# Moving the single-tile case to the head of each expert's code in a routed MoE kernel

## The chip, the core and the metric

## The reference

Attention over 8 batches with 8 heads (keys and values pooled by 8) gives 4608 rows of 512; each row is then sent to one of 8 experts.

```
scores = scale * np.matmul(q, k_p.transpose(0, 1, 3, 2))
...
logits = x @ w_gate
e_idx = np.argmax(logits, axis=1)
...
for e in range(E):
    mask = e_idx == e
    ...
    h = np.maximum(x[mask] @ w1[e], 0.0)
    ye = h @ w2[e]
    out[mask] = gate_w[mask, None] * eom[mask, e, None] * ye
```

w1[e] is 512 x 1024, w2[e] is 1024 x 512. Which expert gets how many rows is known only at run time. With the inputs that are timed the experts e0 to e7 get 1018, 55, 333, 239, 827, 724, 24 and 1388 rows, that is 8, 1, 3, 2, 7, 6, 1 and 11 tiles of 128 rows.

## The kernel before

Attention and routing take the first 176 us or so. At their end DVE works out a small integer table from the counts (`job_table`, L700): for each expert how many jobs of three tiles (trips) and of two tiles (pairs) it has, and some flags. Every engine then loads its words of this table and branches on them.

The experts run in order. A trip or a pair is one job: its tiles are transposed (PE's input `xt` is made by DVE from `turned`, high parts by ACT, low parts by DVE), PE runs the first layer (`l1`, L1055, weights `w1a` or `w1b`) and the second layer (L1032, weights `w2a` or `w2b`), DVE and ACT make `ht` between them, and DVE scales the result to `rows` (L1306). The letters a and b are two buffers that alternate between experts: e0, e2, e4, e6 use a for w1 and w2, the odd experts use b. Weights come in chunks to `stage` and are split into a high and a low part by ACT (L1171) and DVE (L1284, a `TENSOR_TENSOR` of 128x1024 each); this goes on during the jobs of the expert before.

An expert with one tile is a lone tile. If it has at most 64 rows, it is also "halved": high and low parts share one tile (`stack`, L1328, copies the low part beside the high one), the weights are the moving operand (L1064), the sums are turned back by PE (L1070), DVE adds halves (L1337) and makes the low part (L1341), the second layer has 16 matmuls (L1041), and DVE ends with three operations (`y_part`, L1299 to L1303). With these inputs e1 and e6 are halved lone tiles. The last tile's scaling of a job (`last_output`, L1308) is done by DVE at the head of the next job, before its first low part `low` of `ht` (L1317), which PE waits for in the second half of `l1`: four of the eight slices of `p_h` fit, the fifth needs the first `ht`.

The code of an expert is written out once per expert for DVE, ACT and POOL; PE has one copy for e0 and one loop over the pairs e1, e2; e3, e4; e5, e6; e7. An expert's code holds first the loop over trips and then the loop over pairs, and the lone tile's code lies inside the pairs' body, behind its `If`s. A lone tile therefore jumps over the trips. PE has three static hints that a branch's target will be needed (`BRANCH_PREFETCH_HINT`); DVE and ACT have none. In a lone tile the split of the weights that come next is done in part before the sums (`AHEAD[1]` chunks, L64) and the rest after the `xt` of the next job (`rest`, L900).

## Time and profile before

| what | value |
|---|---|
| median of 3 runs | 604.85 us (603.19 to 605.37) |
| the profiled execution | 606.75 us, its span 605.0 us |
| PE busy | 570.1 us, 94% of the span |
| DVE, ACT, POOL busy | 362.5, 256.5, 224.2 us |
| mean granted clock of PE | 0.994 |

The span is the time between the first and the last recorded instruction of the profiled execution; 1.75 us of its time lie outside. Times of rows are counted from the span's start. An idle time in brackets stands ahead of the instruction and names what ended it; "issue" means that the engine waited for nothing that the profile shows, so for its own sequencer.

### The profile page before, as it was taken

What the parts mean: (1) busy time and instruction counts of PE and PEld (TensorE: products, weight loads), DVE (VectorE), ACT (ScalarE), POOL (GpSimd) and SP (SyncE); (2) the same over time, 40 slices, a digit from 0 to 9 for tenths busy, and PEclk for the clock granted to TensorE, in tenths of its full rate; (3) what the DMA queues carried; (4) which work ended last, traced back from release to release, by engine and by line L of the source; (5) the groups of instructions that cost most, each with busy time, mean ns of one, the idle gap of its engine ahead of it and who ended that gap; (6) DMA issues with size and microseconds to landing.
All of it is one profiled execution on the core that took longest, in us unless ns stands there. A gap on an engine that the chain in (4) does not pass through costs nothing.

```text
span 605.0 us, 11705 instructions
## 1 busy us (share of the span) xinstructions
PE 570.1 (94%) x3331; PEld 510.9 (84%) x3331; DVE 362.5 (60%) x880; ACT 256.5 (42%) x701; POOL 224.2 (37%) x331
## 2 busy tenths in 40 slices
PE   2998999999999999879999999999999899999996
PEld 2898898888878989579889898998997788989895
DVE  6788899988978625678586423574254652232323
ACT  2897888788525204438254111542041420302120
POOL 2958879851634312144123131222112431213121
PEclk9999999999999999979999999999999999999999
DMA  8766888976567443678666203372125202010110
GB/s 333 301 250 266 349 309 306 382 293 150 187 205 192 155 105 113 180 208 273 195 234 207 62 36 73 109 231 55 52 87 144 62 16 77 8 52 19 35 36 35
DMA packets 44682, 96.59 MB, mean 160 GB/s; under 512 B 5515, under 2 KB 28475, under 8 KB 41664
## 3 DMA queue, kind: packets, MB, share of 16 engines
q1 hardware_dynamic: 29328, 48.95, 25.2%
q10 hardware_dynamic: 7488, 27.27, 13.6%
q0 software_dynamic: 7792, 19.61, 9.2%
q14 instruction: 55, 0.45, 0.2%
q8 instruction: 19, 0.31, 0.2%
HBM read 76.36 MB, written 22.91 MB: 164 GB/s over the span
## 4 chain that ended last, share of the span: by engine, by line
PE 62%; issue 3%; DVE 2%; DVEq 1%; DMA 1%; SPq 1%; ACT 1%; POOL 0%; ACTq 0%; POOLq 0%
PE p_h L1055 31%; PE p_y L1032 30%; DMA rows<-xs 1%; PE p_h L1064 1%; DVE turned L1260 0%; DVE w2b L1284 0%; DVE q_even L1337 0%; PE p_h L1070 0%; DVE w2a L1284 0%; DVE xt L1256 0%; DVEq L1309 0%; SPq L988 0%; ACT xt L1160 0%; ACT q_even L1193 0%; DVE rows L1306 0%
## 5 line engine op out<-in xcount | busy, mean ns | idle before, releaser
L1182 ACT ACTIVATE ht<-p_h 128x384 fp32r<-128x384 f32 (+1 forms) x104 | 46.8, 450 | 253.2 <-PE p_h L1055 250.8
L1483 POOL DMA_INDIRECT out<-rows,dst x41 | 42.9, 1045 | 217.1 <-DVE rows L1306 209.4
L1317 DVE SCALAR_TENSOR_TENSOR ht<-p_h,ht 128x384 fp32r<-128x384 f32 (+1 forms) x104 | 52.2, 504 | 97.3 <-ACT ht L1182 97.3
L1055 PE MATMUL p_h<-xt,w1b 128*128 128x384 f32 (+1 forms) x672 | 107.5, 321 | 1.0 <-DVE ht L1317 0.6
L1055 PEld LDWEIGHTS p_h<-xt,w1b 128*128 128x128 f32 x672 | 106.3, 188 | 2.3 <-DVE ht L1317 0.9
L1032 PE MATMUL p_y<-w2b,ht 128*128 128x512 f32 x456 | 107.4, 395 | 0.0
L1032 PEld LDWEIGHTS p_y<-w2b,ht 128*128 128x128 f32 x456 | 85.4, 188 | 20.1
L1055 PE MATMUL p_h<-xt,w1a 128*128 128x384 f32 (+1 forms) x576 | 88.3, 315 | 4.3 <-issue 3.9
L1055 PEld LDWEIGHTS p_h<-xt,w1a 128*128 128x128 f32 x576 | 87.5, 194 | 5.5 <-issue 4.3
L1032 PE MATMUL p_y<-w2a,ht 128*128 128x512 f32 x384 | 88.4, 390 | 0.0
L1032 PEld LDWEIGHTS p_y<-w2a,ht 128*128 128x128 f32 x384 | 71.9, 188 | 14.6
L1306 DVE TENSOR_SCALAR rows<-p_y,sc 128x512 f32<-128x512 f32 x39 | 28.9, 744 | 86.8 <-PE p_y L1032 77.0
L289 ACT ACTIVATE p<-p_h,m 128x72 f32<-128x72 f32 x288 | 69.7, 346 | 16.6 <-DVE m L283 16.2
L311 PE MATMUL p_y<-vbd,pT 128*128 128x162 f32 (+3 forms) x400 | 68.8, 320 | 5.8 <-DVE xg L334 4.1
L1458 POOL DMA_INDIRECT rows<-xs,src x51 | 55.5, 1089 | 24.9 <-POOL src L1454 13.5
L311 PEld LDWEIGHTS p_y<-vbd,pT 128*128 128x128 f32 (+1 forms) x400 | 54.2, 180 | 11.2 <-issue 3.7
L446 POOL DMA_INDIRECT xs<-xg,where x36 | 36.8, 1022 | 39.2 <-DVE grec L328 19.3
L203 POOL TENSOR_TENSOR kq<-kq 128x288 f32<-128x288 f32 (+1 forms) x63 | 42.3, 677 | 16.8 <-DMA kq<-kT 11.4
L277 PE MATMUL p_h<-kbd,q_even 128*128 128x144 f32 (+1 forms) x160 | 29.6, 315 | 11.5 <-DMA q_even<-qT 8.8
L334 DVE TENSOR_TENSOR xg<-p_y,grec 128x240 f32<-128x240 f32 x72 | 35.3, 490 | 1.4
L277 PEld LDWEIGHTS p_h<-kbd,q_even 128*128 128x128 f32 (+1 forms) x160 | 23.6, 197 | 13.9 <-issue 9.6
L1260 DVE STREAM_TRANSPOSE turned<-rows 128x512 f32<-128x512 f32 x51 | 32.4, 686 | 4.8 <-DMA rows<-xs 2.0
(190 smaller groups left out, 688.6 us busy)
## 6 DMA issues: line engine op xcount, KB each, us to landing
stage<-wst ACTq DMA_DIRECT2D x52, 512.0 KB, 4.3
rows<-v SPq DMA_DIRECT2D x8, 1280.0 KB, 6.4
kq<-kT SPq DMA_DIRECT2D x7, 1152.0 KB, 11.8
rows<-xs SPq DMA_DIRECT2D x36, 192.0 KB, 4.8
stage<-wst SPq DMA_DIRECT2D x12, 512.0 KB, 6.0
kq<-qT SPq DMA_DIRECT2D x4, 1152.0 KB, 9.4
q_even<-qT SPq DMA_DIRECT2D x3, 1152.0 KB, 10.3
rows<-xs SPq DMA_DIRECT2D x20, 128.0 KB
```

Source lines behind the costliest of these rows:

```text
L203: eng.tensor_tensor(k[:, :, 0:w], k[:, :, 0:w], k[:, :, w:2 * w], op=ALU.add)
L277: nc.tensor.matmul(s[r0:r0 + n, 144 * c:144 * c + 144], q_t[b][:, 2 * a + c, s0:s0 + n], kbd[b % 2][:, 2 * a + c, :], start=True, stop=True)
L289: nc.scalar.activation(pt[i % 3][:, o:o + KEYS], sv[:, h], AF.Exp, bias=m[:, h:h + 1])
L311: nc.tensor.matmul(av[r0:r0 + n, COLS * h:COLS * (h + n_heads)], pT[:, c, r0:r0 + n], vbd[b % 2][:, slot:slot + n_heads].rearrange("p h f ...
L334: nc.vector.tensor_tensor(xg[g][:, j, 0:LEAD + DM].rearrange("p (f h) -> p f h", h=H)[:, :, hs], avv[:, :, 0:GATE + D].rearrange("p h f -> ...
L446: ins = nc.gpsimd.indirect_dma_start(out=whole_rows(xs), out_offset=bass.IndirectOffsetOnAxis(ap=where, axis=0), in_=x.bitcast(I32), in_of ...
L1032: i = mm(to, ht[:, h, f, P * k:P * k + P], w[:, part, o:o + DM], start=(f == 0 and part == 0 and h == 0), stop=(f == 7 and h == 1))
L1055: i = mm(p_h[f % DEEP][:, 0:n], w[:, part, o:o + P], xt[:, x, d, 0:n], start=(d == 0 and part == 0 and x == 0), stop=(d == 3 and part == 1))
L1182: act(ht[:, 0, f, 0:size * P], p_h[f % DEEP][:, 0:size * P], AF.Relu).then_inc(q["hh"], 1)
L1317: nc.vector.scalar_tensor_tensor(ht[:, 1, f, 0:n], src, 0.0, ht[:, 0, f, 0:n].bitcast(F32), op0=ALU.max, op1=ALU.subtract).then_inc(q["hl" ...
L1458: nc.gpsimd.indirect_dma_start(out=xm[:, k].bitcast(I32), out_offset=None, in_=xs, in_offset=bass.IndirectOffsetOnAxis(ap=src[:, k:k + 1], ...
L1483: nc.gpsimd.indirect_dma_start(out=out, out_offset=bass.IndirectOffsetOnAxis(ap=dst[:, k:k + 1], axis=0), in_=yb[2 if k == size - 1 else k ...
```

## The change

For DVE, ACT and PE's looped experts an expert's code now begins with a branch on "lone": the lone tile's body stands there, its last jump goes to the end of the expert's code, and a hint for that jump's target stands at the start of the body. All experts with more tiles branch over the lone body to `many`, which holds trips and pairs. Five hints stand in PE's stream, eight each in DVE's and ACT's. `AHEAD[1]` falls from 2 to 1, `stack()` moves from the job before a lone tile to the lone tile's own start, a semaphore ("hv") is merged into another ("ad"), and the flag for at most 64 rows is made from the count alone, which drops `sh.halved` (32 bytes per partition) and some small steps of the table. The second weight buffers lie 32 bytes lower: `w1b` from 158112 to 158080, `w2b` from 190880 to 190848, while `w1a` (41600) and `w2a` (74368) stay.

```
-AHEAD = {3: 8, 2: 8, 1: 2}
+AHEAD = {3: 8, 2: 8, 1: 1}
...
+        few = t([P, E], F32, "few")
+        v_.tensor_scalar(few, cnt, float(P // 2), None, op0=ALU.is_le)
...
-        v_.scalar_tensor_tensor(spare, tiles, float(P), cnt, op0=ALU.mult, op1=ALU.subtract)
-        yield 0
-        v_.tensor_scalar(spare, spare, float(P // 2), float(HALF), op0=ALU.is_ge, op1=ALU.mult)
...
-        v_.scalar_tensor_tensor(sh.halved, sh.single, 0.0, spare, op0=ALU.is_gt, op1=ALU.mult)
+        v_.scalar_tensor_tensor(sh.single, few, float(HALF), sh.single, op0=ALU.mult, op1=ALU.add)
...
-    v_.tensor_tensor_scan(rest[:, ::-1], none[:, ::-1], sh.halved[:, ::-1], 0.0, op0=ALU.mult, op1=ALU.add)
     v_.tensor_tensor(table[:, E + 1:E + 2], after[:, 0:1], full, op=ALU.add)
     v_.memset(table[:, E:E + 1], 0)
-    yield 0
-    v_.tensor_tensor(pairs, pairs, sh.halved, op=ALU.add)
-    yield 0
-    v_.scalar_tensor_tensor(pairs[:, 0:E - 1], rest[:, 1:E], 2.0, pairs[:, 0:E - 1], op0=ALU.mult, op1=ALU.add)
...
+        if lone and not (lone == "half" and isinstance(e, int)):
+            name = f"lone_{nc.next_id()}"
+            branch = eng.br_cond((v & (HALF + 64)) <= HALF if lone == "half" else single <= 0, f"{name}_many", f"{name}_body")
+            if hint is not None and hint[LONE[1]] is not None:
+                branch.branch_hint(hint[LONE[1]])
+                hint[LONE[1]] = None
+            with nc.body(f"{name}_body", valid_engines=[eng.engine]):
+                end = eng.mark_branch_hint_location()
+                body(e, 2, job, slot, True if lone == "half" else v & HALF, 0, after_pairs, 1, late)
+                eng.br(f"{name}_end").branch_hint(end)
+            with nc.body(f"{name}_many", valid_engines=[eng.engine]):
+                many(job, slot)
+                eng.br(f"{name}_end")
+            nc.switch_bb(f"{name}_end")
+        else:
+            many(job, slot)
...
+            if e and single is not None:
+                with eng.If(single > 0):
+                    stack()
             with eng.If(job > 0):
                 last_output(u)
...
-            if e + 1 < E:
-                with eng.If(last * 1024 + halves[1] > 1024):
-                    stack()
...
-        sh.slots, sh.upto, sh.single, sh.halved = (sb(n, [P, E], F32) for n in ("slots", "upto", "single", "halved"))
+        sh.slots, sh.upto, sh.single = (sb(n, [P, E], F32) for n in ("slots", "upto", "single"))
```

The order of instructions at three places follows. The first is DVE's tail of e6's lone tile, between the `xt` of e7's first job and the turns for the one after it. Before, two chunks of weights are split there:

```order
L924 COMPARE_AND_BRANCH
L1284 TENSOR_TENSOR w2b<-stage2,w2b 128x1024
L1284 TENSOR_TENSOR w2b<-stage3,w2b 128x1024
L924 UNCONDITIONAL_BRANCH
L1266 ISA
```

In the changed kernel it is three (the line numbers are those of the changed kernel):

```order
L935 COMPARE_AND_BRANCH
L1295 TENSOR_TENSOR w2b<-stage1,w2b 128x1024
L1295 TENSOR_TENSOR w2b<-stage2,w2b 128x1024
L1295 TENSOR_TENSOR w2b<-stage3,w2b 128x1024
L935 UNCONDITIONAL_BRANCH
L1277 ISA
```

One split moved from in front of the halves' sums to this place; turns and `y_part` stand behind it.

The second place is DVE's way into e7 (L799 reads the expert's word, L781 branches to trips or past them, and L1306 is `last_output`). Before, the trips' code follows in line:

```order
L945 UNCONDITIONAL_BRANCH
L799 REGISTER_ALU x2
L781 COMPARE_AND_BRANCH
L807 UNCONDITIONAL_BRANCH
L807 ISA
L1355 ISA
L1355 COMPARE_AND_BRANCH
L1309 ISA x5
L1306 TENSOR_SCALAR rows<-p_y2,sc 128x512
```

In the changed kernel the word is read at L793, and L812 branches to `many`; between them and the trips stands the whole lone body, which begins like this:

```order
L962 UNCONDITIONAL_BRANCH
L793 REGISTER_ALU x2
L812 COMPARE_AND_BRANCH
L817 BRANCH_PREFETCH_HINT
L1367 REGISTER_ALU
L1367 COMPARE_AND_BRANCH
L1340 ISA x4
L1341 CAST xt<-xt 128x4x64
L1367 UNCONDITIONAL_BRANCH
```

An expert with many tiles now takes the branch L812 over that body. Counted by instruction addresses in the built program, e7's branch lies at about 2839 to 2860 and its `many` at 2920; e2's lie at 1276 to 1300 and 1371, and the lone tiles of e1 and e6 begin at 994 and 2549 in line with the expert before.

The third place is PE's head of a looped expert (the first of the two in an iteration). Before, trips follow the header:

```order
L781 COMPARE_AND_BRANCH
L807 UNCONDITIONAL_BRANCH
L807 ISA
L1023 ISA
L1055 MATMUL p_h0<-xt,w1b 128x384 x12
```

In the changed kernel the lone tile follows it:

```order
L812 COMPARE_AND_BRANCH
L817 BRANCH_PREFETCH_HINT
L1090 REGISTER_ALU
L1040 ISA
L1094 ISA
L1081 MATMUL p_h0<-w1b,xt 128x512 x8
```

PE's lone tile is entered without a jump, and a trip or pair lies further from the header than before.

## Rows read from the trace of the kernel before

**Rows 1.** The page, part 1: busy time and share of each engine
```profile
PE 570.1 (94%) x3331; PEld 510.9 (84%) x3331; DVE 362.5 (60%) x880; ACT 256.5 (42%) x701; POOL 224.2 (37%) x331
```

**Rows 2.** PE's timeline at e1 and e2: start, us, line, operation, [idle before]
```profile
246.86 2.82 PE L1064 MATMUL p_h<-w1b,xt 128*128 128x512 f32 x11 [1.58 <-issue]
...
252.18 0.66 PE L1070 MATMUL p_h<-ident,q_even 128*128 128x128 f32 x4 [0.69 <-ACT q_even L1193]
...
260.99 19.54 PE L1055 MATMUL p_h<-xt,w1a 128*128 128x384 f32 x96 [3.90 <-issue]
```

**Rows 3.** Windows at e1's end: us, busy times (x count), granted clock, DMA
```profile
257.00:259.00 2.00, 0.09 (x1) 0.00 (x0) 2.00 (x3) 0.56 (x1) 1.54 (x1) 1.00 0.95 389
...
260.00:266.00 6.00, 5.01 (x16) 5.01 (x17) 4.01 (x7) 0.77 (x2) 2.43 (x4) 0.50 0.67 140
```

**Rows 4.** PE's timeline: both layers of a trip with either buffer
```profile
335.96 16.52 PE L1032 MATMUL p_y<-w2a,ht 128*128 128x512 f32 x72
430.59 16.81 PE L1055 MATMUL p_h<-xt,w1b 128*128 128x384 f32 x96
447.24 16.95 PE L1032 MATMUL p_y<-w2b,ht 128*128 128x512 f32 x72
```

**Rows 5.** PE's timeline in the attention, an idle of middle length
```profile
12.78 2.29 PE L277 MATMUL p_h<-kbd,q_even 128*128 128x144 f32 x8 [2.73 <-ACT kbd L208]
```

**Rows 6.** PE's timeline at e6 and e7
```profile
464.03 2.68 PE L1064 MATMUL p_h<-w1a,xt 128*128 128x512 f32 x11
468.00 0.66 PE L1070 MATMUL p_h<-ident,q_even 128*128 128x128 f32 x4 [1.30 <-ACT q_even L1193]
...
470.89 0.66 PE L1070 MATMUL p_h<-ident,q_even 128*128 128x128 f32 x4 [1.07 <-ACT q_even L1193]
...
476.17 8.60 PE L1055 MATMUL p_h<-xt,w1b 128*128 128x384 f32 x48 [0.41 <-DVE xt L1256]
485.38 8.61 PE L1055 MATMUL p_h<-xt,w1b 128*128 128x384 f32 x48 [0.61 <-DVE ht L1317]
```

**Rows 7.** The chain of waits, e5 to e7: start, us, what (q: an engine's sequencer)
```profile
459.87 0.06 DVEq L781
459.93 4.25 issue
...
481.58 0.06 DVE rows L1303
...
482.39 0.04 DVEq L781
...
484.11 0.07 DVE rows L1306
```

**Rows 8.** DMA queues from 450 to 485 us: packets, MB, share
```profile
q14 instruction: 9, 0.07, 0.6%
```

**Rows 9.** The page, part 5: second-layer matmuls by weight buffer
```profile
L1032 PE MATMUL p_y<-w2b,ht 128*128 128x512 f32 x456 | 107.4, 395 | 0.0
L1032 PE MATMUL p_y<-w2a,ht 128*128 128x512 f32 x384 | 88.4, 390 | 0.0
```

**Rows 10.** DVE's timeline at the end of the job table
```profile
167.75 0.16 DVE L730 TENSOR_TENSOR jobs<-jobs,halved 128x8 f32<-128x8 f32 x1
...
167.95 0.17 DVE L732 SCALAR_TENSOR_TENSOR jobs<-jobs 128x7 f32<-128x7 f32 x1
```

**Rows 11.** DVE's timeline from e1's lone tile into e2
```profile
255.16 1.90 DVE L1256 TENSOR_TENSOR xt<-turned,xt 128x512 fp32r<-128x512 f32 x3 [0.49 <-ACT xt L1160]
256.98 2.35 DVE L1284 TENSOR_TENSOR w2a<-stage,w2a 128x1024 fp32r<-128x1024 f32 x2
...
262.63 0.49 DVE L1303 TENSOR_SCALAR rows<-rows,sc 64x512 f32<-64x512 f32 x1
264.30 0.75 DVE L1306 TENSOR_SCALAR rows<-p_y,sc 128x512 f32<-128x512 f32 x1 [1.19 <-issue]
265.75 0.56 DVE L1317 SCALAR_TENSOR_TENSOR ht<-p_h,ht 128x384 fp32r<-128x384 f32 x1 [0.70 <-ACT ht L1182]
```

## The prediction

> **What bounds the kernel now.** I read the page first: TensorE is busy for 570.1 us, 94% of the span [rows 1]. So only three things can move the time by much: the pace of its matmuls, its idle gaps, and its clock. Next I read PE's timeline around the two lone tiles, where the changed code lies. At e1 PE idles 1.58 us before its first matmul and, behind the lone tile, 3.90 us before e2's first layer, both ended by "issue", that is by its own sequencer [rows 2]. [...] e2's first 96 matmuls then take 19.54 us [rows 2], where the same number of the same form takes 16.81 [rows 4]: 2.73 us. A gap of 2.73 us elsewhere is followed by matmuls at their usual pace [rows 5]. At e6 and e7 the gaps are 1.30, 1.07, 0.41 and 0.61 us [rows 6].

> The chain of waits says why e6 is slow: DVE stands 4.25 us at the branch over the trips (L781) for nothing but its sequencer, while the same branch, when the target follows in line, takes 0.04 us [rows 7]. Instruction packets move in that stretch, nine with 0.07 MB [rows 8], so about 8 KB each. By addresses in the built program the long waits of DVE and ACT lie where a branch passes an address 64 past a multiple of 128, so I take a packet for a block of 128 instructions that begins there, and the 4.25 us for a branch into a block that has not arrived: at e6 DVE had entered the block that it leaves only half a microsecond before.

> **The change, part by part.**

> *Second weight buffers, 32 bytes lower.* The second layer reads w2b at 395 ns a matmul and w2a at 390 [rows 9]; for a trip's 72 matmuls that is 16.95 against 16.52 us, 0.43 or, with its neighbours, 0.42 us [rows 4], while the first layer shows no such difference. The buffers differ in address: w2a lies on a multiple of 128 bytes, w2b 32 bytes past one; after the change both lie on one. If that is the cause, 456 matmuls gain 456/72 x 0.42 = 2.66 us. Bounds: 0 (the cause is something else) and 2.7. I take 2.66, since nothing else in the two stretches differs.

> *Shorter table.* Two dependent steps go, of some 0.2 us each (167.75 to 167.95 is one) [rows 10], and five or so small operations of 0.16. It runs under attention's matmuls; what shows is the time at which the table can be loaded. Against it DVE and ACT now branch over e0's lone body. I take +0.2, bounds -0.3 and +0.5.

> *e1.* The lone tile is now in line behind e0 on PE, DVE and ACT, so the idle of 1.58 us [rows 2] goes and everything in e1 shifts by that. The lone tile's last jump is hinted, so the 3.90 us go too. PE could begin e2 when its xt is there: 255.16 + 1.90 - 1.58 = 255.48 [rows 11], with the branches about 256.4. After 48 matmuls (8.6 us, as the first half at e7 takes [rows 6]) it needs DVE's first ht, at 265.0.

> DVE is then the question. It has one split more behind the sums (AHEAD 1 instead of 2): 2.35/2 = 1.18 us [rows 11]. Its last y_part operation starts at 262.63 - 1.58 + 1.18 = 262.2; `last_output` follows 1.67 us later and takes 0.75, the first low part 0.56 [rows 11]: done about 265.2 by DVE alone, 266.2 with the longer header and ACT's part. PE would idle about 1.2 us.

> But behind the lone tile's hinted end DVE now must branch over e2's own lone body, where the trips stood in line before. The end lies at 1276, `many` at 1371, in the next block of 128. [...] This is the same place in a block's life as the branch of e6 before, so the price is from that row: 4.25 us [rows 7], less the half microsecond that the header takes anyway, 3.7. Bounds: 0 (the block is there) and 4.25. I take 3.7, so the first low part is done at about 269.0. PE then idles from 265.0 to 269.0 and ends the layer at 277.6, where it was 260.99 + 19.54 = 280.53 [rows 2]: +2.9 us. If its clock falls in that gap, 2.73 of it are lost again. The gap of 4.0 us lies at the 3.90 that was followed by a fall [rows 2, 3] and above the 2.73 that was not [rows 5]; as the headers' time in my sum is rounded up, I take no fall, almost evenly.

> *e3.* PE's looped code has grown, and e3's pair lies a block further from the header. Before, PE had no idle at e3; now it may have to fetch that block. Bounds: 0, and 3.90 as the largest idle ended by issue [rows 2]. I take the middle, -2.0.

> *e6 and e7.* DVE's 4.25 us and ACT's like it go, so e6's turns come without the 1.30 and most of the 1.07 us [rows 6]: by e1's own measure, from the first matmul to the second turn 252.18 - 246.86 = 5.32 us [rows 2], the second turn comes at 464.03 + 5.32 = 469.35 instead of 470.89 [rows 6], 1.54 earlier. The third split costs 1.18 of it on DVE, the longer header some 0.6: without a stall e7's first low part is about 0.3 late. With the stall (e6's end at 2839, e7's `many` at 2920, again the next block) it is 0.3 + 3.7 less the 0.5 counted twice in the header, 3.5 us late: PE's second half starts at 485.38 + 3.5 = 488.9 [rows 6]. PE, which starts e7's first layer 1.5 us earlier (474.7) and has 8.6 us to do [rows 6], idles from 483.3 to 488.9. That is 5.6 us, more than the 3.90 that was followed by a fall: 2.73 more. Sum -6.2. Without the stall -0.3.

> *The rest at nothing.* `stack()` (one copy) moves to e6's and e1's start on DVE, which arrives there well before PE's first matmul once its stall is gone; without that cover it costs its own 0.3 us. The merged semaphore removes waits of no length. ACT branches into a next block at e7 too, but its part for e7 is behind DVE's.

> The sum: 2.66 + 0.2 + 2.9 - 2.0 - 6.2 = -2.4 us, a loss. The profiled execution took 606.75 us (span 605.0), 1.9 above the median of 604.85; taken as a difference and set on the median it gives **607.3 us**.

> [...]

> **Rivals.**

> 1. *The forecast (chance 0.30):* DVE stalls at both heads, the clock falls at e7 alone: 607.3; its own range is 604.5 to 608.5, from e3's term and the stall's length.
> 2. *No stall on DVE (0.25), the other side:* the hint, or the fetch that goes on behind it, has brought the next block before DVE arrives. e2's layer then ends at about 256.4 + 16.81 + 1.2 + 0.2 = 274.6, 5.9 earlier; e7 loses 0.3. Sum 2.66 + 0.2 + 5.9 - 2.0 - 0.3 = +6.5: 598.4. It decides when the block arrives within a microsecond or so of the end being entered. For it: the hint is given some 10 us ahead. Against: DVE's branch at L781 waited 4.25 us for a next block [rows 7].
> 3. *The clock falls at e2 too (0.22):* 2.7 more: 610.0. For it: a gap as long as that of 3.90.
> 4. *Stalls, but no fall of the clock at either (0.08):* 2.66 + 0.2 + 2.9 - 2.0 - 3.5 = +0.3: 604.6. Against: the gap at e7 would be longer than the one that was followed by a fall.
> 5. *The address is not why w2b is slower (0.15):* the first term is nothing, and the change to w2b does not do anything: 610.0 with the first case, 601.1 with the second.

> **How the numbers follow.** The likeliest case gives 607.3. The range reaches to the second and third: 598.0 to 610.3; beyond it remain the worst of the fifth and third, and the best of the second with no stall at e3. Half a per cent, 3 us, is about what a measurement of this kernel tells from no change, so faster means under 601.8 and slower over 607.9. Faster: the second case nearly whole, with a part of the fifth and of the fourth, 0.31. Same: two thirds of the first, most of the fourth, a little of each other, 0.36. Slower: the third, a third of the first, most of the fifth, 0.33.

> **What would show it.** L1032 with w2b (its line number changes) at 390 ns shows the address right, 395 wrong. PE's idle ahead of e1's first matmul and ahead of e2's first layer gone shows the lone head and the hint right. A DVE idle by issue of 3 to 4 us between y_part and `last_output`, at e2 and at e7, shows the stall; then PE's fifth slice waits for DVE's ht, for 4 to 5.6 us, and the windows behind show a clock of 0.50 or not. A gap at e3's first matmul by issue shows the third term. The prediction is wrong if DVE passes both heads in under a microsecond; or if the attention, which the edit should leave alone, moves by a microsecond or more.

## The result, and the profile after

The changed kernel takes 612.45 us (median of 4 runs, 611.85 to 615.3) against 604.31 for the one before (4 runs): ratio 1.0144, interval 1.0106 to 1.0183. That is 8.1 us slower, on the side of the loss that was forecast but outside the range, which ended at 610.3. The profiled execution took 611.85 us, its span is 610.1 (605.0 before), its granted clock 0.988 (0.994).

PE's timeline of the changed kernel, with the idle time ahead of a group in brackets, answers to [rows 2, 4, 6]:

```profile
190.56 16.93 PE L1072 MATMUL p_h<-xt,w1a 128*128 128x384 f32 x96 [1.58 <-DVE xt L1267]
246.10 2.65 PE L1081 MATMUL p_h<-w1b,xt 128*128 128x512 f32 x11
256.56 8.61 PE L1072 MATMUL p_h<-xt,w1a 128*128 128x384 f32 x48 [0.48 <-issue]
271.89 10.00 PE L1072 MATMUL p_h<-xt,w1a 128*128 128x384 f32 x48 [6.72 <-DVE ht L1328]
300.72 13.27 PE L1072 MATMUL p_h<-xt,w1b 128*128 128x256 f32 x96 [2.47 <-issue]
452.29 16.52 PE L1049 MATMUL p_y<-w2b,ht 128*128 128x512 f32 x72
479.08 8.59 PE L1072 MATMUL p_h<-xt,w1b 128*128 128x384 f32 x48 [0.42 <-DVE xt L1267]
490.41 9.99 PE L1072 MATMUL p_h<-xt,w1b 128*128 128x384 f32 x48 [2.74 <-DVE ht L1328]
```

In the kernel before, the same views have these rows for the starts of e0 and e3 and for DVE's way into e7:

```profile
189.59 16.91 PE L1055 MATMUL p_h<-xt,w1a 128*128 128x384 f32 x96 [0.42 <-DVE xt L1256]
296.74 11.52 PE L1055 MATMUL p_h<-xt,w1b 128*128 128x256 f32 x96
484.11 0.75 DVE L1306 TENSOR_SCALAR rows<-p_y,sc 128x512 f32<-128x512 f32 x1 [2.04 <-issue]
```

The two idle times that the change was to remove are gone: none ahead of e1 (1.58 before), 0.48 ahead of e2 (3.90 before). Inside e2's first layer stands a new one of 6.72 us, ended by DVE's `ht`; there are others ahead of e3 (2.47) and inside e7's first layer (2.74). e0 begins at 190.56 after waiting 1.58 for `xt` (189.59 and 0.42 before). The second layer with w2b takes 16.52 us for a trip, like w2a's in [rows 4].

DVE's timeline of the changed kernel at e2 and e7 answers to [rows 11] and [rows 7]:

```profile
262.65 0.49 DVE L1314 TENSOR_SCALAR rows<-rows,sc 64x512 f32<-64x512 f32 x1
270.62 0.75 DVE L1317 TENSOR_SCALAR rows<-p_y,sc 128x512 f32<-128x512 f32 x1 [7.48 <-issue]
271.29 0.55 DVE L1328 SCALAR_TENSOR_TENSOR ht<-p_h,ht 128x384 fp32r<-128x384 f32 x1
...
489.14 0.75 DVE L1317 TENSOR_SCALAR rows<-p_y,sc 128x512 f32<-128x512 f32 x1 [2.96 <-issue]
```

At e2 DVE stands 7.48 us for its own sequencer between `y_part` and `last_output`, 1.19 before. At e7 it is 2.96 against 2.04. The chain of waits of the changed kernel (start, us, what) has one piece of it:

```profile
264.31 5.42 issue
...
298.25 2.47 issue
```

The first begins as the branch past e2's lone body is taken, the second is PE's idle ahead of e3. The windows (us, busy of PE, PEld, DVE, ACT, POOL, granted clock, DMA share, GB/s) show the clock behind the three gaps, as [rows 3] did behind one:

```profile
266.00:268.00 2.00, 0.00 (x0) 0.00 (x0) 0.00 (x0) 0.28 (x1) 0.00 (x0) 1.00 1.06 291
270.00:272.00 2.00, 0.11 (x1) 0.11 (x1) 1.38 (x3) 0.00 (x0) 0.00 (x0) 0.50 0.06 18
272.00:274.00 2.00, 2.00 (x7) 2.00 (x8) 2.00 (x3) 0.56 (x2) 1.66 (x1) 0.50 0.08 8
303.00:306.00 3.00, 3.00 (x17) 3.00 (x16) 1.94 (x3) 1.77 (x3) 0.31 (x2) 0.55 0.64 186
490.00:492.00 2.00, 1.59 (x5) 1.59 (x6) 1.75 (x4) 0.00 (x0) 1.01 (x1) 0.50 0.00 0
```

So the granted clock falls from 1.00 to 0.50 at e2, e3 and e7 (0.55 is the mean of a window with 2.7 of its 3 us at 0.50). At e2 and e7 the 48 matmuls behind the gap take 10.00 and 9.99 us, not 8.6; e3's 96 take 13.27, where 11.52 or 11.68 is usual for that form.

Where the difference between the two profiled executions arises, counted on PE from one landmark to the next (plus is a loss): start of e0 +0.97 (189.59 to 190.56); e0's start to e2's second layer +0.39; from there to e3's second layer +4.36; the second layers with w2b -2.45 in all; e6's first matmul to e7's second layer +1.79. The sum is 5.06, PE's last second layer ending at 605.24 (594.17 + 11.07) instead of 600.18 (588.82 + 11.36). The other 3 us of the 8.1 are not in these two traces: the profiled execution of before lies 2.44 above its own median, that of after 0.6 below.

### The profile page after: what moved, and what is told of

It is laid out like the page before. It is cut to its first block, busy times and chain, and to the rows that moved or that the text cites. A ratio compares the mean times of both kernels' runs of the same rounds, so it can differ in the third digit from the quotient of the medians.

```text
span 610.1 us, 11593 instructions
## 1 busy us (share of the span) xinstructions
PE 569.7 (93%) x3331; PEld 513.3 (84%) x3331; DVE 361.1 (59%) x876; ACT 256.5 (42%) x701; POOL 228.3 (37%) x331
## 4 chain that ended last, share of the span: by engine, by line
PE 61%; issue 4%; DVE 3%; DVEq 1%; DMA 1%; ACT 1%; SPq 1%; POOL 0%; ACTq 0%; POOLq 0%
PE p_y L1049 30%; PE p_h L1072 29%; PE p_h L1081 1%; DMA rows<-xs 1%; DVE turned L1271 1%; PE p_h L1087 0%; DVE w2a L1295 0%; DVE xt L1267 0%; SPq L1005 0%; DVE w2b L1295 0%; DVE rows L1312 0%; DVE q_even L1348 0%; DVE rows L1310 0%; ACT q_even L1204 0%; DVEq L1320 0%
## 5 line engine op out<-in xcount | busy, mean ns | idle before, releaser
L1072 PE MATMUL p_h<-xt,w1b 128*128 128x384 f32 (+1 forms) x672 | 110.8, 326 | 5.6 <-DVE ht L1328 2.7
L1072 PEld LDWEIGHTS p_h<-xt,w1b 128*128 128x128 f32 x672 | 109.4, 194 | 7.2 <-issue 3.7
L1049 PE MATMUL p_y<-w2b,ht 128*128 128x512 f32 x456 | 104.8, 390 | 0.0
L1072 PEld LDWEIGHTS p_h<-xt,w1a 128*128 128x128 f32 x576 | 86.2, 192 | 10.2 <-DVE ht L1328 7.0
L283 DVE TENSOR_REDUCE m<-p_h 128x4 f32<-128x288 f32 x72 | 32.3, 448 | 3.9 <-PE p_h L277 3.6
```

The source lines that it names most:

```text
L1049: i = mm(to, ht[:, h, f, P * k:P * k + P], w[:, part, o:o + DM], start=(f == 0 and part == 0 and h == 0), stop=(f == 7 and h == 1))
L1072: i = mm(p_h[f % DEEP][:, 0:n], w[:, part, o:o + P], xt[:, x, d, 0:n], start=(d == 0 and part == 0 and x == 0), stop=(d == 3 and part == 1))
```

## The experiments

Each kernel is compared with the kernel before on the same chip, whose median was 604.1 to 605.1 us.

**Four kernels, each with one part of the changed kernel undone or moved.**

The buffers back where they were (a_back):

```
-        sb("pad", [P, 24], F32)
+        sb("pad", [P, 32], F32)
```

> The changed kernel with 32 bytes more in front of the second weight buffers, so that they lie where they lay before (w2b 32 bytes past a multiple of 128); nothing else. Theory (the address is why w2b was slower): the second layer's matmuls with w2b go from 390 ns back to 395, five trips cost 0.42 us more each and two pairs 0.28, so about 2.7 us slower than the changed kernel. Rival (something else in the change made them faster): they stay at 390 ns and the time stays.

616.66 us, ratio 1.0192 (1.0166 to 1.0219), against 1.0144 (1.0106 to 1.0183) for the changed kernel: 0.48% or 2.9 us of ratio, where 2.7 was expected. The two intervals overlap, so the pace of the matmuls decides here and not the time. The line of the second layer in this kernel (matmuls by operand, least, median and greatest ns):

```profile
L1049 PE MATMUL p_y<-w2b,ht x456: 389/394/398, 315.5 to 609.1; 128*128 128x512 f32 x152
L1049 PE MATMUL p_y<-w2a,ht x384: 387/389/398, 183.1 to 404.3; 128*128 128x512 f32 x192
```

w2b's matmuls are slower again (median 394 ns), w2a's are not (389). The rival falls.

DVE's later code 68 places on (a_pad68), by instructions in a branch that is never taken here (it is for an e0 without rows); and the same with 40 (a_pad40). The line that declares the semaphore `pad` is left out:

```
...
                 split(plan(e, 0) + further(e))
+                for _ in range(68 if e == 0 and eng.engine == nc.vector.engine else 0):
+                    eng.nop().then_inc(q["pad"], 1)
```

> The changed kernel with 68 instructions that are never executed in DVE's code between e0 and e1. All of DVE's later code moves by 68 places, so that the end of e1's lone tile (1344) and e2's many (1439) lie in one block of 128 (1344 to 1471). Theory (DVE's 5.4 us at e2's head are a branch into a block not yet fetched): that wait falls under 1 us, PE's gap in e2's first layer falls from 6.7 us to about 1.5, its clock does not fall there, and the time falls by 5 to 8 us. Rival (DVE waits there for something that the code's place does not touch): the wait stays at 5 us and the time within 1.5 us.

606.83 us, ratio 1.0035 (1.0013 to 1.0057): 1.1% less than the changed kernel. DVE's and PE's rows at e2:

```profile
265.44 0.75 DVE L1319 TENSOR_SCALAR rows<-p_y,sc 128x512 f32<-128x512 f32 x1 [2.12 <-issue]
```

```profile
266.71 8.59 PE L1074 MATMUL p_h<-xt,w1a 128*128 128x384 f32 x48 [1.48 <-DVE ht L1330]
```

The 7.48 us fell to 2.12, PE's gap from 6.72 to 1.48, and the second half takes 8.59 us, so the clock stays. Nothing but the place of DVE's code was changed. The 2.12 that remain are no stall: the chain has 0.14 us behind the branch in place of 5.42, and the way into e2 is longer by some 0.9 us (1.19 before), as at e7 (2.96 against 2.04). Another branch now comes off badly: at e6's head DVE stands 4.52 us (1.82 in the changed kernel), which costs PE 0.22 us.

> The same with 40 instructions: the end of e1's lone tile (1316) and e2's many (1411) still lie in two blocks, as at e7, where the changed kernel showed no wait; and as at e6, the lone body itself (1034 to 1104) now runs over a block's end (1088). Theory A (a branch into the next block waits whenever the block of the end was entered just before): DVE's wait at e2's head stays at 4 to 5.5 us, the time stays. Theory B (a lone body that runs over a block's end has the block behind the hinted one fetched early, as at e7): the wait falls under 1 us and the time falls by 5 to 8 us, as with 68.

611.31 us, ratio 1.0120 (1.0087 to 1.0153). DVE's row at e2:

```profile
270.35 0.75 DVE L1319 TENSOR_SCALAR rows<-p_y,sc 128x512 f32<-128x512 f32 x1 [7.40 <-issue]
```

Moved by 40, the end (1316) and `many` (1411) still lie in two blocks by the estimate of 128 places, and DVE stands as long as unmoved (7.48). Theory B falls: a lone body that runs over a block's end does not help. Theory A holds at e2. It does not explain e7: by the same estimate the branch to `many` leads into a next block there, but it waits 0.14 us in the changed kernel, and DVE idles no more here than there (2.94 against 2.96).

AHEAD[1] at 2 (a_ahead2):

```
-AHEAD = {3: 8, 2: 8, 1: 1}
+AHEAD = {3: 8, 2: 8, 1: 2}
```

> The changed kernel with AHEAD[1] back at 2, so that DVE and ACT split two chunks ahead of the lone tile's sums and two behind, not one and three. Theory (the third split behind the sums makes DVE late by 1.18 us at e2's and e7's first ht): DVE is 1.2 us earlier there, PE's gap at e7 falls from 2.7 to about 1.5 us, at e2 from 6.7 to about 5.5, if the sums do not come later for it; 2 to 4 us faster with the clock kept at e7. Rival (a second split ahead of the sums makes them late by as much): the turns of e1 and e6 wait about 1 us longer, and the time stays within 1 us.

607.42 us, ratio 1.0041 (1.0019 to 1.0063), 1.0% less than the changed kernel, more than expected. PE's rows at e7 and the window behind:

```profile
478.15 8.61 PE L1072 MATMUL p_h<-xt,w1b 128*128 128x384 f32 x48 [0.46 <-DVE xt L1267]
488.31 8.60 PE L1072 MATMUL p_h<-xt,w1b 128*128 128x384 f32 x48 [1.55 <-DVE ht L1328]
```

```profile
490.00:492.00 2.00, 2.00 (x13) 2.00 (x13) 0.56 (x1) 0.49 (x1) 0.08 (x1) 1.00 0.02 0
```

The gap at e7 falls from 2.74 to 1.55, by the third split's 1.19, and with it the clock's fall goes (8.60 instead of 9.99 us). So a split of 1.2 us cost 2.6 at e7 alone. At e2 the gap falls to 5.03, and the clock still falls. In this trace it does not fall at e3 (11.78 us behind a gap of 3.03), at which the edit does not aim; how much of the 1.0% is owed to the split is therefore not shown beyond e7.

**Parts alone, and parts together.**

The lower buffers alone, in the kernel before (b_shift: the pad there 16 instead of 24):

> The kernel before with only one part of the change: the second weight buffers 32 bytes lower (by a smaller pad). Theory (the address alone makes the second layer with w2b slower): w2b's matmuls fall from 395 to 390 ns, and the time by 2.7 us, to about 601.9; nothing else moves. Rival (it is the changed order or something else that made them faster): 395 ns, no change.

602.99 us, ratio 0.9974 (0.9957 to 0.9990), a gain of 1.6 us with 0.6 to 2.6 in the interval; the 2.7 expected lie just outside.

```profile
L1032 PE MATMUL p_y<-w2b,ht x456: 387/389/398, 306.4 to 595.7; 128*128 128x512 f32 x152
```

The pace follows the address in both kernels, 389 against 394 ns with the changed code and 389 against 395 with the code before, so this part of the change gains in both. A little is given back: the first layer of a pair with w1b takes 11.68 us here and in the changed kernel (e7's), 11.52 in the kernel before and in a_back (e7's), 0.3 us for two pairs.

The same, with one hint on PE (b_shift_hint), the lone code left inside the pairs:

```
...
-                with eng.If(halves[0] > 0):
+                name = f"half_{nc.next_id()}"
+                eng.br_cond(halves[0] <= 0, f"{name}_pair", f"{name}_body")
+                with nc.body(f"{name}_body", valid_engines=[eng.engine]):
+                    end = eng.mark_branch_hint_location()
                     l1_rows(e, u, job, ((0, 0), (1, 0)), begin_l2)
                     l2_part(e, job)
                     no_tile(e)
-                with eng.Else():
+                    eng.br(f"{name}_end").branch_hint(end)
+                with nc.body(f"{name}_pair", valid_engines=[eng.engine]):
                     pair()
+                    eng.br(f"{name}_end")
+                nc.switch_bb(f"{name}_end")
...
```

> The same, and PE's halved lone tile in the looped code gets its last jump hinted at its start, with the lone code where it lay before. Theory (the 3.90 us of PE's idle ahead of e2 are the fetch of that jump's target, and the fall of the clock follows from them): the idle there falls under 1 us; PE then waits for DVE's first ht in e2 less than 2 us; the clock stays, and e2's first layer ends some 5 us earlier: about 597. Rival (the target's block alone does not help, since the next is missing, or the idle moves to DVE's ht with the same length): the gap moves into the layer, the time stays at 602.

597.69 us, ratio 0.9902 (0.9863 to 0.9940), the fastest kernel of the study: 6 us under the kernel before by the ratio (7 by the medians), some 15 under the changed one. PE's row at e2, first of b_shift, without the hint, then with it:

```profile
259.11 19.54 PE L1055 MATMUL p_h<-xt,w1a 128*128 128x384 f32 x96 [3.25 <-issue]
...
257.20 16.90 PE L1055 MATMUL p_h<-xt,w1a 128*128 128x384 f32 x96 [0.50 <-DVE xt L1262]
```

The idle (3.90 in the kernel before, 3.25 in b_shift) and the clock's fall are both gone, and the layer has no new gap: DVE, whose code is as before, idles 1.19 us by issue between `y_part` and `last_output` (7.48 in the changed kernel), and its first `ht` is in time.

Both repairs of DVE (a_pad68_ahead2):

> The changed kernel with both: DVE's code 68 places on, and AHEAD[1] back at 2. Theory (the stall at e2 and the third split are two separate losses): e2's layer has a gap under 1 us, e7's gap is 1.5 us and its clock is kept; with e3's gap left, about 602 us, that is 10 less than the changed kernel. Rival (the two gains overlap, since the clock falls in one place or another): about 605 to 607, no faster than either alone.

603.41 us, ratio 0.9977 (0.9963 to 0.9991): 1.67% less than the changed kernel, where the two alone gave 1.09 and 1.03. Most of both adds up. The rival falls. PE's row at e2:

```profile
266.02 8.60 PE L1074 MATMUL p_h<-xt,w1a 128*128 128x384 f32 x48 [0.41 <-DVE ht L1330]
```

The changed kernel without the early hint of the last jump (a_nohint):

```
-                end = eng.mark_branch_hint_location()
...
-                eng.br(f"{name}_end").branch_hint(end)
+                eng.br(f"{name}_end")
```

> The changed kernel without the early hint of the lone body's last jump, on PE, DVE and ACT (eight instructions fewer on DVE and ACT, so the code moves by a few places; the blocks of e1's end and e2's many on DVE stay apart). Theory (the hint brings the end's block in time): at the lone tile's end PE stands 3 to 4 us again before e2, as before the change, DVE waits some 3 to 4 us at the jump besides the 5.4 at many, and the same at e6; 5 to 12 us slower than the changed kernel. Rival (the blocks come in sequence anyway while the lone tile runs): no change within 1.5 us.

618.22 us, ratio 1.0228 (1.0204 to 1.0252): 0.84%, about 5 us, slower than with it. PE's rows at e2 and e7:

```profile
261.25 9.95 PE L1071 MATMUL p_h<-xt,w1a 128*128 128x384 f32 x48 [5.07 <-issue]
...
496.52 10.07 PE L1071 MATMUL p_h<-xt,w1b 128*128 128x384 f32 x48 [8.02 <-DVE ht L1327]
```

DVE's chain of waits, at e2 and then at e7, has a wait at the lone body's last jump, which the hint names, and one at the branch to `many` behind it:

```profile
262.69 4.28 issue
...
267.62 2.30 issue
...
486.49 4.29 issue
...
491.37 2.10 issue
```

With the hint the wait at the last jump is 0.56 us at e2 and 0.48 at e7, so the hint works. What it is worth depends on the branch behind it. At e2 that branch waits 5.42 with the hint and 2.30 without it, so DVE stands 7.48 and 7.68 us in all, and e2's second layer even starts a little later with the hint (281.73 against 280.50). At e7, where the branch to `many` waits 0.14 us with the hint, PE's gap is 2.74 instead of 8.02. Part of that may be the place of the code, since DVE's code lies a few places earlier without the hints; no run separates the two.

**Why e7 had no stall, and the other gaps.**

110 places (a_pad110, the loop above with 110):

> The changed kernel with 110 never executed instructions in DVE's code between e0 and e1. The end of e1's lone tile (1386) and e2's many (1481) lie in two blocks, as in the changed kernel; but the block in which the lone body begins (1088 to 1215) is now entered just before the hint, as at e6 in the changed kernel, where no wait followed, and not 4 us ahead of it. Theory C (a hint that is given while the next block is still on its way has the block behind its target fetched too): DVE's wait at e2's head falls under 1 us, the time by 4 to 6 us against the changed kernel. Theory D (the moment of the hint makes no difference, and e7 has its block early for another reason): the wait stays at 4 to 6 us, the time at 611 to 613.

618.72 us, ratio 1.0235 (1.0211 to 1.0260). PE's rows at e2 and e7:

```profile
271.94 11.19 PE L1074 MATMUL p_h<-xt,w1a 128*128 128x384 f32 x48 [6.84 <-DVE ht L1330]
...
497.10 11.23 PE L1074 MATMUL p_h<-xt,w1b 128*128 128x384 f32 x48 [6.42 <-DVE ht L1330]
```

Theory C falls, since e2's gap stays. DVE's chain of waits at e7 has this piece at the branch to `many`:

```profile
490.27 3.75 issue
```

So e7, which was free of the stall (0.14 us), has it here: its `many` (3030) again lies in the block behind its end's (2949), if blocks are of 128 places, as it did unmoved (2920 and 2839). So the place of the code decides at e7 too, but not by this rule alone. Why e7 passes unmoved, and moved by 40, is open.

The block of 128 is the author's estimate, from packets of 8 KB [rows 8] and places counted in the program. What the runs show at e2 is DVE's idle: 7.48 us with the end at 1276 and `many` at 1371, 7.40 with 1316 and 1411, 7.48 with 1386 and 1481, but 2.12 with 1344 and 1439. Blocks that begin at 1344 and 1472 fit these four; one that begins at 2880 does not fit e7 unmoved.

A hint on PE for e3's branch over the trips (a_e3), on top of a_pad68_ahead2 (`past_trips`, left out here, keeps the branch in hint[5]):

```
...
                 mark(eng, hint, PAIRS)
+                if isinstance(e, tuple) and not e[1]:
+                    hint[5].branch_hint(eng.mark_branch_hint_location())
                 l2(e, u, 2, job)
```

> The changed kernel with 68 places and AHEAD[1] at 2 (603.4 us), and on PE a hint in the last job of the looped expert ahead for the branch over the next expert's trips. Theory (PE's 3.2 us ahead of e3 and the fall of its clock behind them are the fetch of the pairs' block, which the longer code moved out of reach): the idle ahead of e3 falls under 1 us, its first layer takes 11.7 instead of 13.3 us, about 4.5 us faster, 599. Rival (the gap comes from something that e3 waits for anyway, xt or weights): the gap stays and ends by another engine, 603.

603.39 us, ratio 0.9985 (0.9967 to 1.0003): no change, the theory's 4.5 us are excluded. PE's row at e3:

```profile
294.36 13.01 PE L1083 MATMUL p_h<-xt,w1b 128*128 128x256 f32 x96 [3.93 <-issue]
```

The same with e0's lone body behind its trips and pairs on DVE and ACT (a_all):

```
...
+            if isinstance(e, int) and e == 0:
+                with nc.body(f"{name}_many", valid_engines=[eng.engine]):
+                    many(job, slot)
+                    eng.br(f"{name}_end")
             with nc.body(f"{name}_body", valid_engines=[eng.engine]):
...
```

> The same, and for e0 on DVE and ACT the lone body stands behind trips and pairs, so that nothing is jumped over at the start of the experts. Theory (DVE's 1.7 us at that jump are why the first layer of e0 starts late and waits 1.6 us for xt): PE's wait there falls to 0.5 us, about 1.0 us faster than with the hint for e3 alone, 598, about as fast as the kernel before with the lower buffers and one hint. Rival (xt comes from a transfer that ends no earlier): no change.

601.48 us, ratio 0.9955 (0.9940 to 0.9969), 1.9 us under a_e3, where 1.0 was expected; the two intervals just touch. e0's first layer starts with no idle (190.48, behind 1.65 us of idle, in a_e3):

```profile
182.79 5.60 PE L1065 MATMUL p_y<-w2a,ht 128*128 128x512 f32 x24
188.30 16.94 PE L1088 MATMUL p_h<-xt,w1a 128*128 128x384 f32 x96
```

DVE's row for the `xt` that PE waits for, first in the changed kernel, then in a_all:

```profile
188.61 1.89 DVE L1267 TENSOR_TENSOR xt<-turned,xt 128x512 fp32r<-128x512 f32 x3 [1.95 <-issue]
...
186.35 1.89 DVE L1285 TENSOR_TENSOR xt<-turned,xt 128x512 fp32r<-128x512 f32 x3 [0.26 <-ACT xt L1189]
```

So the jump over e0's lone body was the cause of the late start.

PE's code 8 places on (a_all_e3), then 72 (a_all_e3c), by the same means as on DVE:

> The last kernel with eight never executed instructions in PE's code of e0, which move the looped code 8 places on. In the two kernels before, the hint fetched the block that holds the place behind the trips (2873), but e3's pair begins at 2947, and a block of PE (256 addresses) seems to begin at 2880, 64 past a multiple of 256; now both places (2881 and 2955) lie in one block. Theory (e3's gap is the fetch of that block, and the hint missed it by 7 places): the idle ahead of e3 falls from 4.9 us to under 1, its first layer takes 11.7 us at the full clock, about 4 to 6 us faster: 596 to 597. Rival (e3's gap has another cause): idle of 3 us or more ahead of e3 as before, 601.

> The last kernel with 72 instead of 8 never executed instructions in PE's code of e0. Theory (e3's gap is a fetch of the next block, which begins between 2887 and 2947, for example at 2944): the place behind the trips (2945) and e3's pair (3019) now lie in one block, which the hint fetches; the idle ahead of e3 falls under 1 us and the time by 2 to 3 us, to 599 or 600. Rival (not a fetch): idle of 2.5 us or more as before.

602.34 us, ratio 0.9952 (0.9935 to 0.9968), and 601.28 us, ratio 0.9936 (0.9912 to 0.9959): both intervals hold a_all's 0.9955. PE's rows at e3, first of the one with 8, then of the one with 72:

```profile
291.31 11.77 PE L1088 MATMUL p_h<-xt,w1b 128*128 128x256 f32 x96 [2.66 <-issue]
```

```profile
290.98 13.27 PE L1088 MATMUL p_h<-xt,w1b 128*128 128x256 f32 x96 [2.52 <-issue]
```

The gap stays in all of them. In the first the clock did not fall behind it (11.77 us), in the second it did (13.27). In the changed kernel a packet on the instruction queue q8 falls into the gap (DMA queues from 297.4 to 300.6 us: packets, MB, share):

```profile
q8 instruction: 1, 0.02, 2.5%
```

The packet moves from 297.74 to 299.01, and PE goes on at 300.72, 1.71 us after its end. In each of the twelve traces with this gap, whose length runs from 2.47 to 4.93 us, such a packet ends 1.69 to 1.75 us before PE goes on. So by this order in time PE waits there for code. Packets on q8 have 16 KB (24 with 0.39 MB in this trace), those on q14 8 KB (55 with 0.45 MB); that one on q8 is a block of 256 places, and where such a block begins, was the author's estimate. Neither of the two places proved right, and no edit removed the gap, so why the packet comes so late is open.

## Why the prediction was wrong

The loss and its main mechanism were forecast, a stall of DVE behind the lone tile's hinted end, but with a sum that was too small: 2.4 us, where the traces lost 5.06 and the medians 8.1. By the steps of the prediction:

- *Buffers, 2.66.* Right in the cause, a little high in size: 2.45 between the traces, 2.9 in a_back, 1.6 (0.6 to 2.6) in b_shift. The 0.16 us that a pair's first layer loses with w1b was not seen; the prediction looked at trips only.
- *Shorter table, +0.2, with the branch over e0's lone body.* Wrong in sign: e0 begins 0.97 later, and a_all shows that the branch over e0's lone body costs about 1.9, more than the shorter table can give back. The prediction put this branch at a fraction of a microsecond without a row for it, while DVE's stall at the same kind of branch was its main term elsewhere.
- *e1 and e2, +2.9.* This is the step that failed: the price of DVE's way into e2. The idle ahead of e1 and e2 went as said. The stall was there, shown by a_pad68, but DVE's first `ht` let PE go on at 271.89, not at 269.0. The sum was too small in two parts, which are 2.6 of these 2.9 us. The stall was taken from the row at e6 (4.25) less half a microsecond, 3.7; the chain has 5.42. And the longer header, which measures about 0.9 us (2.12 in a_pad68 against 1.19), is missing: 266.2 counts 1.0 for it and ACT's part, but 269.0 is 265.2 + 3.7. With it the gap would have been forecast at about 5.0 instead of 4.0. With a measured gap of 6.72 the fall of the clock, which the prediction left out "almost evenly", came too; it cost 1.39 us (10.00 for 8.61) and not 2.73. Measured: a loss of 0.39 for both experts in place of a gain of 2.9. Why the same kind of branch costs 5.42 here and 3.75 at e7 in a_pad110 was not tested. In each of the two waits one packet of 8 KB moves on the instruction queue q14, 3.30 us after the wait begins at e2 and 1.65 at e7, and DVE goes on 1.75 and 1.57 us after its end. So the difference lies ahead of the packet; no run shows what starts the fetch. From 266 to 268 us the windows give a DMA share of 1.06, so the fetch may have waited behind weights; that is not shown.
- *e3, -2.0.* The idle was near (2.47), the fall of the clock behind it was not foreseen (13.27 for 11.52 us before); the stretch lost 4.36.
- *e6 and e7, -6.2.* Wrong for the better: no stall. PE's gap of 2.74 at e7 was 0.61 before; 1.19 of it is the third split, shown by a_ahead2, and about 0.9 fits the longer header (2.96 against 2.04 us). The clock fell all the same, for 1.39 us; -1.79 in all. The prediction had put the case without a stall at -0.3; nearly all of the missing 1.5 is this fall.
- *The gap taken as safe.* A gap of 2.73 us [rows 5] was read as followed by matmuls at their usual pace, and it stood against a fall at e2. The row does not show it: its eight matmuls take 2.29 us, and four of the same form take 0.66 from 17.73 us on, 0.29 against 0.17 us each. The trace's first record of the granted clock stands at 17.60 us. In the runs gaps of 2.74 and 2.47 were followed by a fall, while 2.66 (a_all_e3), 2.91 (a_pad40) and 3.03 (a_ahead2) were not. The length of a gap does not settle it.
- *The base.* The terms were set on the median of the kernel before as differences from a trace that was itself 2.4 us slower than that median. This is most of the 3 us by which the medians moved more than the traces; the traces' own loss of 5.06, set on the median, would have been 609.9 and inside the range. Part of it shows: in b_shift and b_shift_hint, whose code ahead of e0 is that of the kernel before, e0 starts at 188.55 and 189.26, so its 189.59 in the trace of before is late.

The rival with the clock falling at e2 as well (610.0) was nearest, and its mechanism is what happened at e2. Its number is near by luck: its sum of -5.2 agrees with the traces' -5.06 because the stall that it has at e7 and that did not come (+4.4) balances what it missed at e0, e2 and e3. The rival without a stall (598.4) failed at e2: the lone tile's end and `many` lie less than 100 places apart there, and DVE stood 5.42 us. With the same two at 1344 and 1439 (a_pad68) it stood 0.14. At e7, where the unmoved branch did not stall, the outcome was that rival's.

## What to carry to other kernels

In this kernel the same kind of branch over a lone body took 0.14 us in one place of the code (e7 in the changed kernel, e2 in a_pad68) and 5.42 in another (e2 in the changed kernel). Moving a rare case to the head of every section turns the common case's fall-through into such a branch, on each engine. Look for the jump behind the one you hint, and for the engine that is then late, before you count a removed idle as a gain; here one hint on one engine, with the code left in place and the lower buffers, gave 597.69 us, and the reordering with hints everywhere 612.45. A delay of 1.2 us on a helper engine can cost more than itself: at e7 it was 2.6, since the gap on TensorE that it lengthened was followed by a fall of the clock from 1.00 to 0.50 (without the delay, in a_ahead2, it was not).

## What the runs showed of the hardware

The second layer's matmuls of 512 columns took 389 to 390 ns with w2b on a multiple of 128 bytes (the changed kernel, b_shift) and 394 to 395 with it 32 bytes past one (the kernel before, a_back). Instructions that are never executed, put into DVE's code between e0 and e1, moved the time of the whole kernel by up to 2%: 606.83 us with 68 of them, 611.31 with 40, 618.72 with 110, 612.45 with none. Without the hint DVE waits 4.28 and 4.29 us at the jump that the hint names, with it 0.56 and 0.48; what is gained depends on the branch behind that jump: in all DVE stands 7.68 us at e2 without the hint and 7.48 with it, 8.33 and 2.96 at e7. PE goes on 1.69 to 1.75 us after the end of the packet of code that it waits for at e3 (twelve traces).
